# 16-bit threshold search on VectorE, matmul level ends and recount, and routing steps placed by a build-time estimate, in a gated scan with an eight-expert mixture

## The chip, the cores and the metric

The kernel runs on one core of one Trainium2 chip. The metric is the device time of one execution in microseconds. Before the change three runs took 1270.08, 1270.74 and 1274.23 us; the median is 1270.74 us. One further execution was taken with the profiler.

Five engines work from their own instruction queues: TensorE (PE, with its weight loads shown as PEld), VectorE (DVE), ScalarE (ACT), GpSimd (POOL) and SyncE (SP). An instruction waits on semaphores that other engines raise; whatever stands behind it on its engine waits too.

## The reference, cut to what matters

```python
def _attn_ref(x, f_logit, lower_bound):            # 4 x 5056 x 256
    f = lower_bound + (1 - lower_bound) * sigmoid(f_logit); i = 1.0 - f
    for t in range(S):
        h = f[:, t] * h + i[:, t] * x[:, t]
        y[:, t] = h

def _moe_ref(x, w_gate, w1, w2):                   # N = 20224 tokens, D 256, E 8, F 1024
    logits = x @ w_gate
    for idx in np.argsort(-logits.flatten()):      # greedy, best pair first
        tok, e = idx // E, idx % E
        if assigned[tok] >= 0 or counts[e] >= cap: # cap = N // E = 2528
            continue
        assigned[tok] = e; counts[e] += 1
    for e in range(E):
        out[assigned == e] = relu(x[assigned == e] @ w1[e]) @ w2[e]
```

A gated scan over 5056 steps gives 20224 token rows. Each token goes to one of eight experts. The assignment is greedy over all (token, expert) scores, with exactly 2528 places in each expert, so an expert's list is known only when the threshold is known at which it fills up.

## The kernel before

**Front.** The tokens come in 40 chunks of 512. `sig`, `fwd` and `back` do the sigmoid (ACT), the product with x (POOL), the transposes (PE, L518), the scan (DVE, L530) and the transposition back together with the gate scores (PE, L540 and L541). The rows are stored to a scratch buffer `hbuf` in DRAM by SP. `prep` takes, in small steps between the chunks, each token's best score `M0`, a one-hot `O` of its best expert, and two numbers `KH` and `KL` that hold the upper and the lower 16 bits of the score as a sortable integer.

**A route** (`route(k)`, eight of them) finds which expert fills up next and at which score. `search` does it in eight levels of base 16, four on `KH`, four on the rest `W`. A level has these steps:

- masks: for 160 columns of tokens and 16 thresholds, `MK[:, :, j, :]` says whether a token lies on the better side of threshold j. The 16 thresholds are shared out: DVE (L272) takes 8 to 13 of them, ACT (L308) five or six by a Sign activation each, POOL (L314) one to three in the first route;
- counts: 20 matmuls (L327) of `MK` with `O` add up, per threshold and expert, how many tokens there are;
- the level end: DVE takes the diagonal (`DM` L332, `CR` L333). In the first route two small matmuls follow (`CR` with `tot`, L346; a flag `fl` with `eighth`, L350). In all later routes DVE spreads `CR` to 128x128 (L354), one fp32r matmul (L357) adds it up, and three DVE steps (L359, L361, L362) make the digit. The last level of every route uses L335, L338, L340, L342;
- the next 16 thresholds `TH` (L366).

`assign` then marks the chosen tokens, `compact` turns the marks into a list of row numbers, eight groups of up to three blocks of 128 (matmuls L430, DVE L441 and L442, ACT `junk` L452, DVE `ids` L456; its PSUM tile has one buffer after the first route, so a group's matmuls wait for the ACT steps of the group before). `update` masks the filled expert in the scores (L464) and counts again how full every expert is: two comparisons (L467), two reductions (L471) and one matmul (L474). For the routes after the first, `argmax` and `keys` do again over 160 columns what `prep` did.

**The mixture.** `moe` goes through the experts in the order in which the routes find them. An expert's 20 tiles of 128 tokens form five chunks of four tiles, six (2, 4, 4, 4, 4, 2) for the first expert. For each chunk and each of eight blocks j of F, `first` does six matmuls into `pw` (L732; weights and tokens are split into a high and a low part) and ACT and DVE make `hh` (L737) and `hl` (L738); `second`, three blocks later, does 12 matmuls into `py` (L754). One block of a four-tile chunk is 6 + 12 matmuls. At a chunk's end ACT copies `y` (L760) and POOL scatters it to the output (L766). POOL also gathers the next tokens (`gather`, L704) and the next expert's weights (`load_w`, L657 and L658); `split` makes the weights' high and low parts (`w1h` L683, `w2s` L681 on ACT, `w1l` L689 on DVE). `trans` transposes the gathered tokens (L719, `xh`, `xl`).

**What sets the order.** The first route runs alone, with nothing to hide it but matmuls on zeros that keep PE busy (`busy`, L288; BZ says how many). The other routes run in the background of the mixture: `search` and the rest are generators that `yield` between steps, and `tick` is called once or twice in each `first` and between the tiles of a `second`. A tick advances each generator by at most one step. Before the change, each `yield` carries a letter, and the table `WAIT` (or `WAIT_1` for the first two routes) says how many ticks pass before the next step:

```python
WAIT = dict(a=2, k=0, m=2, c=6, d=2, z=1, g=0, f=0, s=4, p0=2, p1=1, p4=7, q0=5, q1=1, q2=7, u=3, w=0)
```

`gather(k + 1, 0)` stands in the second block of an expert's last chunk (GJ) and forces, by `ids_of`, as many steps of `compact` as its list still lacks; `gather(k + 1, 1)` stands four blocks later. The tile framework then schedules the instructions of the mixture on each engine; so the order of the queues is not exactly that of the calls, and is read from the built program below.

## Time and profile before

| | before |
|---|---|
| median of 3 runs | 1270.74 us (1270.08 to 1274.23) |
| the profiled execution's own time | 1270.02 us |
| its span, first to last instruction | 1268.2 us |
| PE, DVE, ACT, POOL busy | 1194.0, 826.9, 620.2, 487.7 us |
| front (scan), until the first route's counts | 0 to 157.8 us |
| first route and first weights, alone | 157.8 to 214.5 us |
| experts 0 to 4, with routes 1 to 6 in the background | 214.5 to 904.9 us: 156.8, 134.7, 133.3, 137.2, 128.4 |
| expert 5, with what is left of the routing | 904.9 to 1025.0 us: 120.1 |
| expert 6, no routing at all | 1025.0 to 1142.0 us: 117.0 |

The stretches begin with an expert's first matmul of L732. Some 1.8 us of the profiled execution's time lie outside its span. In the views a row gives start and length of an instruction, the engine, the line and the tiles (out<-in); what stands in brackets is the idle time before it and who ended that. "PEclk" is the TensorE clock that was granted: 1.00 is full speed, 0.50 is half. A busy PE is one that has a matmul in flight, which is not the same as one at its peak.

### The profile page before, as it was taken

The numbers are of one execution on the slowest core, as the hardware profiler recorded it, in microseconds if no ns is written. First come the engines' busy times: TensorE is split into PE (matmuls) and PEld (weight loads), VectorE is DVE, ScalarE is ACT, GpSimd is POOL, SyncE is SP. The second block draws the span as 40 slices with busy tenths as digits, with TensorE's granted clock in tenths as the row PEclk, the third lists the DMA queues.
The fourth block names the chain that finished last, engine by engine and source line by source line (L and its number), as shares of the span: only waits on it lengthen the run. The fifth ranks groups of instructions, "written<-read, shape, count | busy, mean of one in ns | idle before, by whom it ended". The sixth has DMA issues, their size and how long they took to land.

```text
span 1268.2 us, 23156 instructions
## 1 busy us (share of the span) xinstructions
PE 1194.0 (94%) x9062; PEld 1080.4 (85%) x9062; DVE 826.9 (65%) x1900; ACT 620.2 (49%) x1386; POOL 487.7 (38%) x467
## 2 busy tenths in 40 slices
PE   7999985999879989999989999999999999999998
PEld 7999964888778878888978888888888989999998
DVE  6999967778857787688679678868633352222222
ACT  7888733543455445355445545553644352322322
POOL 6677544512443242344243224333432342322312
PEclk9999996999889989999999999999999999999999
DMA  9999972201221211121131113112221111111100
GB/s 339 360 354 362 345 230 85 76 18 53 69 66 41 84 56 34 46 95 50 42 113 37 35 35 117 39 47 101 76 83 43 43 50 42 47 39 42 42 18 33
DMA packets 51725, 123.13 MB, mean 97 GB/s; under 512 B 7968, under 2 KB 28192, under 8 KB 50592
## 3 DMA queue, kind: packets, MB, share of 16 engines
q0 software_dynamic: 18816, 58.87, 14.7%
q1 hardware_dynamic: 32256, 62.78, 14.1%
q8 instruction: 71, 1.16, 0.4%
q14 instruction: 38, 0.31, 0.1%
q10 hardware_dynamic: 544, 0.01, 0.0%
HBM read 79.56 MB, written 42.07 MB: 96 GB/s over the span
## 4 chain that ended last, share of the span: by engine, by line
PE 47%; DVE 5%; ACT 2%; issue 1%; DMA 1%; POOL 0%; POOLq 0%; ACTq 0%; DVEq 0%
PE py L754 22%; PE pw L732 21%; DVE hl L738 1%; PE pt L719 1%; PE rt L327 1%; DMA r<-in_moe_w_dram,wi 1%; DVE w1l L689 1%; ACT w1h L683 1%; PE rt L430 0%; ACT hh L737 0%; ACT MK L308 0%; DVE w2s L687 0%; ACT junk L452 0%; DVE xl L723 0%; POOL out_dram L766 0%
## 5 line engine op out<-in xcount | busy, mean ns | idle before, releaser
L754 PE MATMUL py<-w2s,hh 128*128 128x256 f32 (+1 forms) x2560 | 493.7, 289 | 3.1 <-ACT y L760 3.1
L754 PEld LDWEIGHTS py<-w2s,hh 128*128 128x128 f32 (+1 forms) x2560 | 409.9, 189 | 28.6 <-issue 7.4
L738 DVE SCALAR_TENSOR_TENSOR hl<-pw,hh 128x512 fp32r<-128x512 f32 (+3 forms) x336 | 221.2, 658 | 292.7 <-ACT hh L737 270.8
L737 ACT ACTIVATE hh<-pw 128x512 fp32r<-128x512 f32 (+3 forms) x336 | 191.2, 569 | 435.6 <-PE pw L732 368.9
L754 PE MATMUL py<-w2s,hl 128*128 128x256 f32 (+1 forms) x1280 | 364.1, 284 | 0.7 <-issue 0.7
L766 POOL DMA_INDIRECT out_dram<-y,ids x160 | 166.2, 1039 | 433.5 <-ACT y L760 385.2
L732 PE MATMUL pw<-xl,w1h 128*128 128x512 f32 (+3 forms) x672 | 261.6, 389 | 3.1 <-DVE xl L723 3.1
L732 PE MATMUL pw<-xh,w1h 128*128 128x512 f32 (+3 forms) x672 | 260.0, 388 | 1.7 <-ACT xh L722 1.7
L732 PE MATMUL pw<-xh,w1l 128*128 128x512 f32 (+3 forms) x672 | 261.2, 389 | 0.0
L704 POOL DMA_INDIRECT xg<-hbuf,ids x160 | 172.7, 1079 | 211.5 <-PE pt L719 119.0
L754 PEld LDWEIGHTS py<-w2s,hl 128*128 128x128 f32 (+1 forms) x1280 | 242.1, 189 | 0.3 <-issue 0.2
L732 PEld LDWEIGHTS pw<-xh,w1l 128*128 128x128 f32 x672 | 129.4, 192 | 23.8 <-issue 0.8
L732 PEld LDWEIGHTS pw<-xl,w1h 128*128 128x128 f32 x672 | 129.4, 193 | 20.4 <-DVE xl L723 4.5
L732 PEld LDWEIGHTS pw<-xh,w1h 128*128 128x128 f32 x672 | 129.2, 193 | 15.1 <-ACT xh L722 2.3
L506 POOL TENSOR_TENSOR xl<-fl,xl 128x1024 f32<-128x1024 f32 (+1 forms) x40 | 94.6, 2366 | 39.9 <-ACT fl L505 28.9
L452 ACT ACTIVATE junk<-rt,r 128x158 bf16<-128x158 f32 x158 | 61.8, 391 | 78.2 <-DVE r L442 51.2
L530 DVE TENSOR_TENSOR_SCAN g<-fg,g,pb 128x512 f32<-128x512 f32 (+4 forms) x78 | 92.9, 1228 | 6.4 <-ACT fg L522 5.9
L540 PE MATMUL pr<-iw,g 128*128 128x136 f32 x316 | 62.7, 280 | 0.0
L541 PE MATMUL pr<-iw,g 128*128 128x136 f32 x316 | 62.5, 279 | 0.0
L522 ACT ACTIVATE fg<-pf,one,nomlb 128x512 f32<-128x512 f32 (+1 forms) x80 | 57.5, 769 | 2.3 <-PE pf L518 0.4
L327 PE MATMUL rt<-O,MK 128*128 128x64 bf16 x1120 | 43.5, 195 | 13.8 <-POOL MK L314 8.7
L327 PEld LDWEIGHTS <-MK 128*128 128x128 bf16 x1120 | 36.7, 99 | 23.2 <-POOL MK L314 10.9
(203 smaller groups left out, 1481.2 us busy)
## 6 DMA issues: line engine op xcount, KB each, us to landing
hbuf<-hr SPq DMA_DIRECT2D x39, 528.0 KB, 9.1
fl<-in_f_logit_dram SPq DMA_DIRECT2D x39, 512.0 KB, 6.0
xl<-in_x_dram SPq DMA_DIRECT2D x39, 512.0 KB, 6.3
xg<-hbuf,ids POOLq DMA_INDIRECT x160
out_dram<-y,ids POOLq DMA_INDIRECT x160
r<-in_moe_w_dram,wi POOLq DMA_INDIRECT x24
hbuf<-hr SPq DMA_DIRECT2D x1, 264.0 KB, 9.2
fl<-in_f_logit_dram SPq DMA_DIRECT2D x1, 256.0 KB, 6.0
```

What stands on the lines that cost most here:

```text
L327: nc.tensor.matmul(ps[:, :64], MK[:, g], O[:, 8 * g:8 * g + 8, :], start=(g == 0), stop=(g == NG - 1))
L452: last = nc.scalar.activation(junk, p3[:, b, :NT], AF.Sign, bias=r[:, 0, b:b + 1], scale=-1.0, accum_out=r[:, 1, b:b + 1])
L506: nc.gpsimd.tensor_mul(XT[i][:np_], FT[i][:np_], XT[i][:np_])
L530: nc.vector.tensor_tensor_scan(GT[i][:, h, c:e], f[:, h, c:e], pb[h][:, c:e], init, op0=OP.mult, op1=OP.add)
L540: nc.tensor.matmul(pr[:, :P + E], g[:, 0], iw[:, :P + E], start=True, stop=False, skip_group_check=True)
L541: nc.tensor.matmul(pr[:, P:], g[:, 1], iw[:, P + E:], start=False, stop=True, skip_group_check=True)
L704: st = nc.gpsimd.indirect_dma_start(out=XG[k, c][:n, q].bitcast(F32), out_offset=None, in_=hbuf, in_offset=ids_at(k, c, q, n))
L732: nc.tensor.matmul(ps[:, :w], a[:, h, j], b[:, h, :w], start=(i == 0), stop=(i == 5))
L737: nc.scalar.activation(hh[:, :w], ps[:, :w], AF.Relu)
L738: v.scalar_tensor_tensor(hl[:, :w], ps[:, :w], 0.0, hh[:, :w].bitcast(F32), op0=OP.max, op1=OP.subtract)
L754: nc.tensor.matmul(py, x, w, start=(j == 0 and i == 0 and q % 2 == 0), stop=(j == FB - 1 and i == 2), skip_group_check=True)
L766: st = nc.gpsimd.indirect_dma_start(out=out, out_offset=ids_at(k, c, r, n), in_=y[:n, r % 2], in_offset=None)
```

## The change

**16-bit keys and thresholds, all masks on VectorE.** The key's upper half is kept as int16 (`K16`), the rest as int16 (`R16`), and the thresholds as an int16 tile of 16 x 8 in which each threshold stands eight times. A level's masks become two DVE instructions of 1280 elements each (80 columns, 16 thresholds), with int16 in and bfloat16 out. ACT and POOL make no masks any more. In the last level threshold 0 is done apart, in fp32 (`wth`). `TH` and `PRE` grow from 16 to 128 elements. Two more DVE steps make `R16` from `W` once per search.

**Short level end.** All routes use the two small matmuls (`CR` with `tot`, `fl` with `eighth`); the spread to 128x128, its fp32r matmul and the three DVE steps behind it go, save in the last level.

**Recount by matmuls.** `update` counts how many tokens lie above the threshold by 20 matmuls of the marks `SB` with `O` and one small matmul, in place of the two comparisons and two reductions.

**Steps issued by an estimate.** `Pace` keeps, while the program is built, an estimate of when each engine is free and each tile ready. A generator's `yield` names an engine and the tiles that the next step needs; a tick takes the step only when the estimate says that the tiles are ready by the time the engine is free, and that this engine is at most 3 us (SLACK) behind PE. The wait tables go. The weight split starts 30 ticks after `load_w`, not 40, with 8 ticks between its pieces unless the next expert is near. Since every call goes through a helper, all instructions have the line L100 in the changed kernel.

```diff
+    def cost(self, eng, op, out, ins, accum):
+        n = self.cols(out)
+        if eng == "PE":
+            moving = ins[-1]
+            if moving.dtype == F32:
+                return 1.71 * n + 4 if op == "matmul" else 0.85 * n
+            return max(29.0, 0.453 * n + 4) if moving.dtype == F32R else max(29.0, n / 2.4 + 2.5)
...
+        if eng == "DVE":
...
+            if all(x.dtype in (BF, I16) for x in (out, *ins)):
+                n /= 2
+            return 145 + 1.045 * n * (2 if "scan" in op else 1) + 80 * accum
+        return 1000.0 if "dma" in op else 200 + 2.3 * n
...
+    def due(self, eng, tiles, slack):
+        now = self.free["PE"]
+        at = max(now, self.free[eng])
+        return at - now <= slack and all(self.ready.get(self.key(t), 0.0) <= at for t in tiles)
...
+    def masks(val, th, c0, c1, j0=0):
         n = (c1 - c0) // 8
+        v.tensor_tensor(MK[:, c0 // 8:c1 // 8, j0:, :],
                         val[:, c0:c1].rearrange("p (g c) -> p g c", c=8).unsqueeze(2).to_broadcast(
+                            [P, n, 16 - j0, 8]),
+                        th[:, j0:].unsqueeze(1).to_broadcast([P, n, 16 - j0, 8]), op=OP.is_ge)
...
-    BZ = [18, 5, 12, 42]
+    BZ = [11, 5, 12, 42]
...
-                    for i in range(3):
-                        for j in ac[2 * i:2 * i + 2]:
-                            nc.scalar.activation(MK[:, :, j, :], val.rearrange("p (g c) -> p g c", c=8), AF.Sign,
-                                                 bias=th[:, j:j + 1], scale=-1.0)
...
+                    for c in (0, 80):
+                        if c and not first:
+                            yield 'DVE',
+                        masks(val, th, c, c + 80, 1 if last else 0)
+                        if last:
+                            v.tensor_scalar(MK[:, c // 8:c // 8 + 10, 0, :],
+                                            W[:, c:c + 80].rearrange("p (g c) -> p g c", c=8), wth, None, op0=OP.is_le)
...
+                yield 'PE', CR
+                nc.tensor.matmul(ps[:, 64:64 + E], tot_v, CR, start=True, stop=True)
+                yield 'DVE', ps
+                v.tensor_scalar(FL, ps[:, 64:64 + E], 0.0, 0.0, op0=OP.is_ge, op1=OP.max, accum_out=fl)
+                yield 'PE', fl
+                nc.tensor.matmul(ps[:, 80:81], eighth, fl, start=True, stop=True)
...
+        if first:
+            v.tensor_scalar(TR, A1, code, None, op0=OP.is_equal)
+            v.scalar_tensor_tensor(MS, W, tlo, TR, op0=OP.is_lt, op1=OP.mult, accum_out=cS)
+        else:
...
-        for e in (0, 4):
-            with nc.allow_low_precision(reason=EXACT):
-                v.tensor_reduce(Qb[:, e:e + 4], TMP[:, :, e:e + 4].rearrange("p c e -> p e c"), AX.X, OP.add)
-            yield 'u'
         ps = rt.tile([P, 512], F32, name="rt")
-        nc.tensor.matmul(ps[:, :E], ones_b, Qb, start=True, stop=True)
+        for g in range(NG):
+            nc.tensor.matmul(ps[:8, :64], SB[:, 8 * g:8 * g + 8], O[:, 8 * g:8 * g + 8, :], start=(g == 0),
+                             stop=(g == NG - 1))
...
-    WAITW, WS_ = 40, 2
+    WAITW, WAITS, SLACK = 30, 8, 3000.0
```

Three places in the queues. On DVE, in the first route, one level from the thresholds to the next `DM`, before:

```order
L366 SCALAR_TENSOR_TENSOR TH<-rt,PRE 128x16
L272 TENSOR_TENSOR MK<-KH,TH 128x20x72
L319 TENSOR_SCALAR PRE<-jt_122,TH 128x16
L332 TENSOR_TENSOR DM<-rt,bm 128x64
L333 TENSOR_REDUCE CR<-DM 128x8
```

and after, the same level:

```order
L100 SCALAR_TENSOR_TENSOR TH<-rt,PRE 128x128
L100 TENSOR_TENSOR MK<-K_168,TH 128x1280 x2
L100 SCALAR_TENSOR_TENSOR PRE<-TH,njt_121 128x128
L100 TENSOR_TENSOR DM<-rt,bm 128x64
L100 TENSOR_REDUCE CR<-DM 128x8
```

The one mask instruction with 9 of 16 thresholds has become two with all 16, each for half of the columns; the six instructions on ACT and POOL beside it are gone.

On PE, at the first block of expert 0's last chunk (the one whose matmuls are 128x224), before. `rt` is a group of the list of expert 1, `g1` its mask:

```order
L732 MATMUL pw_4490<-xh_4315,w1l_2951 128x224
L732 MATMUL pw_4490<-xh_4315,w1h_2950 128x224
L732 MATMUL pw_4490<-xl_4316,w1h_2950 128x224
L430 LDWEIGHTS g1_4444
L430 MATMUL rt_4486<-RA_187,g1_4444 128x160
```

and after, at the second block of the same chunk:

```order
L100 MATMUL pw_4319<-xh_4087,w1l_2840 128x224
L100 MATMUL pw_4319<-xh_4087,w1h_2839 128x224
L100 LDWEIGHTS g1_4280
L100 MATMUL rt_4326<-RA_186,g1_4280 128x160
L100 LDWEIGHTS g1_4280
```

Before, this is the fourth group of the list (`rt_4230`, `rt_4312` and `rt_4405` stand earlier, in the chunk of 512); after, it is the first. The next groups after (`rt_4344`, `rt_4396`, `rt_4482`) stand 10, 13 and 39 matmuls of the mixture behind one another.

On ACT, where expert 1's weights are split, before:

```order
L737 ACTIVATE hh_4209<-pw_4202 128x512
L683 ACTIVATE w1h_4377<-r1_4166,omlb_101 128x512 x4
L737 ACTIVATE hh_4237<-pw_4226 128x512
L681 ACTIVATE w2s_4379<-r2_4167 128x2x256 x2
L452 ACTIVATE junk_4255,r_4254<-rt_4230,r_4254 128x158
```

and after:

```order
L100 ACTIVATE hh_4203<-pw_4193 128x512
L100 ACTIVATE w1h_4243<-r1_4211,omlb_101 128x512 x4
L100 ACTIVATE hh_4239<-pw_4232 128x512
L100 ACTIVATE w2s_4245<-r2_4212 128x2x256 x4
L100 ACTIVATE hh_4303<-pw_4294 128x224
L100 ACTIVATE junk_4336,r_4335<-rt_4326,r_4335 128x158
```

Before, fifteen blocks of expert 0 come behind the first piece of the split; after, nine, eight of them in the short last chunk, and all eight pieces stand ahead of the first `junk` step of expert 1's list.

342 lines of the change are left out of this document (181 added, 161 removed).

## The prediction

> **What bounds the kernel now.** I read the table of stretches first, cut at each expert's first matmul; its columns are length, busy time (and instructions) of PE, PEld, DVE, ACT and POOL, granted clock, DMA share, GB/s.
>
> ```profile
> 214.50:371.30 156.80, 139.48 (x1041) 124.73 (x1042) 119.70 (x301) 73.11 (x194) 56.64 (x53) 0.92 0.18 55
> 371.30:506.00 134.70, 128.66 (x984) 113.98 (x983) 101.04 (x252) 68.29 (x174) 44.45 (x43) 0.97 0.17 54
> 506.00:639.30 133.30, 128.12 (x1018) 114.40 (x1017) 101.14 (x244) 67.92 (x168) 47.94 (x45) 1.00 0.18 57
> 639.30:776.50 137.20, 130.09 (x983) 115.40 (x982) 104.42 (x263) 63.14 (x152) 49.55 (x48) 0.98 0.22 68
> 776.50:904.90 128.40, 125.77 (x964) 112.41 (x963) 99.17 (x249) 65.66 (x166) 46.49 (x43) 1.00 0.19 60
> 1025.00:1142.00 117.00, 116.10 (x762) 105.46 (x761) 40.67 (x60) 40.44 (x69) 40.76 (x40) 1.00 0.15 46
> ```
>
> PE carries the mixture. Expert 6, with no routing beside it, takes 117.0 us. Experts 0 to 4 take 690.4 us where five times 117.0 is 585.0, so background routing costs 105 us of PE's time although DVE is busy for only about 75% of these stretches. The waits of PE between 214.5 and 904.9 us say what it stood for (total, times, longest):
>
> ```profile
> PE rt L430 <- ACT junk L452: 6.6, 6, 1.9
> PE rt L474 <- DVE Qb L471: 5.3, 3, 3.1
> PE rt L357 <- DVE ZR L354: 5.1, 5, 1.7
> PE rt L413 <- DVE RS L409: 3.7, 3, 3.2
> PE py L754 <- ACT y L760: 3.1, 2, 2.9
> PE rt L327 <- DVE MK L272: 2.5, 2, 1.5
> PE rt L357 <- DVE CR L333: 1.8, 3, 0.8
> PE pw L732 <- ACT xh L722: 1.7, 2, 1.1
> PE rt L327 <- ACT MK L308: 1.3, 1, 1.3
> ```
>
> These hold 31 us, most of it for routing matmuls that reached the head of PE's queue before the step in front of them was done; the mixture's matmuls stood behind them. The third view is the clock, in the five stretches of this stage where it was cut:
>
> ```profile
> 214.70:224.90 10.20, 8.18 (x38) 7.52 (x38) 8.82 (x24) 3.25 (x11) 6.54 (x5) 0.50 0.19 52
> 323.90:330.70 6.80, 5.79 (x24) 4.88 (x24) 5.43 (x15) 4.34 (x11) 4.20 (x4) 0.50 0.18 61
> 358.00:368.30 10.30, 8.88 (x63) 8.33 (x61) 4.67 (x15) 5.32 (x18) 4.11 (x5) 0.67 0.20 68
> 460.40:467.20 6.80, 6.34 (x23) 5.61 (x24) 5.96 (x18) 3.29 (x11) 5.12 (x5) 0.50 0.22 78
> 661.80:668.60 6.80, 5.21 (x19) 4.71 (x19) 5.40 (x13) 5.77 (x9) 2.59 (x3) 0.50 0.52 182
> ```
>
> Length times the missing share of the clock is 5.1 + 3.4 + 3.4 + 3.4 + 3.4 = 18.7 us. So the 105 us are about 31 of long waits, 19 of clock, and 55 of routing's own matmuls and small gaps. The front, up to 157.8 us, is not touched: the page's slices show the DMA queues full there, and what `prep` saves on DVE lies under the loads.
>
> **The first route, alone on the chip (157.8 to 214.5 us).** Nothing hides it, so each step counts. One level of the timeline, from the thresholds to the next diagonal:
>
> ```profile
> 167.59 0.17 DVE L366 SCALAR_TENSOR_TENSOR TH<-rt,PRE 128x16 f32<-128x16 f32 x1 [0.25 <-PE rt L350]
> 167.80 1.66 DVE L272 TENSOR_TENSOR MK<-KH,TH 128x1440 bf16<-128x1440 f32 x1
> 167.86 1.70 ACT L308 ACTIVATE MK<-KH,TH 128x160 bf16<-128x160 f32 x5 [3.08 <-DVE TH L366]
> 167.93 2.07 POOL L314 TENSOR_SCALAR MK<-KH,TH 128x160 bf16<-128x160 f32 x1 [2.65 <-DVE TH L366]
> 170.06 0.76 PE L327 MATMUL rt<-O,MK 128*128 128x64 bf16 x20 [0.52 <-POOL MK L314]
> 170.86 0.23 DVE L332 TENSOR_TENSOR DM<-rt,bm 128x64 f32<-128x64 f32 x1 [1.11 <-PE rt L327]
> ```
>
> POOL's single threshold ends last, and the 20 matmuls follow: 3.23 us from the start of `TH` to their end. After the change DVE makes two masks of 1280 elements. The trace has no 16-bit instruction with two inputs, so I bound one mask. At the pace of the fp32 masks above (1.66 us for 1440) it takes 1.48 us. The other end is the fastest that DVE goes in this program, where one input is compared with a column:
>
> ```profile
> L422 DVE TENSOR_SCALAR g<-IO,st 128x384 bf16<-128x384 f32 x40 | 16.6, 416 | 0.0
> L359 DVE TENSOR_TENSOR GP<-rt,rE 128x128 f32<-128x128 f32 x42 | 12.1, 288 | 26.4 <-PE rt L357 14.5 <-PE pw L732 9.6 <-PE rt L430 2.0
> L422 DVE TENSOR_SCALAR g<-IO,st 128x128 bf16<-128x128 f32 x8 | 2.2, 278 | 0.0
> L383 DVE TENSOR_TENSOR asg<-asg,TI 128x160 f32<-128x160 f32 x7 | 2.2, 316 | 0.0
> ```
>
> 256 more elements cost 138 ns, 0.54 ns each, so 1280 cost 0.278 + 1152 x 0.00054 = 0.90 us. The row nearest by operation is the fp32 mask, but what the change alters is just what separates the two: half the bytes per element, and thresholds laid out so that no input repeats one element along its innermost run. I take 0.90 us. [...]
>
> A level then is 0.21 us to the masks, 0.11 more because `TH` has 128 elements (row L359, 0.288, against 0.17), 1.80 for two masks, 0.06 to PE, and 0.38 for the second ten matmuls, the first ten running under the second mask: 2.56 us, 0.67 less. With slow masks it is 3.72, 0.49 more. Six levels: -4.0 (slow +2.9). The fewer filler matmuls (18 to 11) end before the masks do and cost nothing. `R16` adds two steps of the kind of row L383: +0.6. `assign` loses two such steps: -0.6. The last level:
>
> ```profile
> 192.50 4.16 POOL L314 TENSOR_SCALAR MK<-W,TH 128x160 bf16<-128x160 f32 x3 [2.74 <-DVE TH L366]
> 196.71 1.25 PE L327 MATMUL rt<-O,MK 128*128 128x64 bf16 x20 [4.69 <-POOL MK L314]
> ```
>
> Three thresholds on POOL and 20 matmuls are 5.5 us from 192.50. After, 0.11 for `TH`, 0.17 for `wth`, two masks of 1200 elements with a piece of 80 each (0.86 + 0.28 at most) and ten matmuls at half clock: 3.2 us, -2.3 (slow -1.2). Sum of this stage: **-6.3 us** (slow +1.7). The stores of the scratch rows do not come late for it, since the page's slices show the DMA queues with room there.
>
> **The background routes.** Five terms, against the 105 us.
>
> *Waits that the change addresses*: L474 5.3 (the recount no longer waits for two reductions), L357 5.1 + 1.8 (the step is gone), L327 2.5 + 1.3, L413 3.7: 19.7 us, and some 1 us of shorter ones. PE now meets these steps when the estimate has them ready. The estimate doesn't see a full PSUM ring, a late DMA or a half clock, so I let a fifth stay: **-17** (0 to -21).
>
> *New work on PE*: seven recounts of 20 matmuls, each about 0.6 us (the 0.76 above less the last one's passage), 4; and in 42 levels a pair of small matmuls in place of one, which on the lone path takes
>
> ```profile
> 171.45 0.39 PE L346 MATMUL rt<-CR,tot 128*128 128x8 f32 x2
> ```
>
> and beside full matmuls I put at 0.1 more than the one removed, 4: **+8** (4 to 20).
>
> *The change of experts 0 to 1 and 1 to 2.* With the steps paced, expert 1's list is begun only in expert 0's short last chunk, behind the whole weight split on ACT. Rows of a split in expert 2, and of a block's matmuls:
>
> ```profile
> 541.35 0.97 POOL L657 DMA_INDIRECT r<-in_moe_w_dram,wi  x1 [4.24 <-DVE wi L379]
> ...
> 549.72 0.97 POOL L658 DMA_INDIRECT r<-in_moe_w_dram,wi  x1 [0.30 <-issue]
> ```
>
> ```profile
> 545.75 2.48 ACT L683 ACTIVATE w1h<-r,omlb 128x512 fp32r<-128x512 f32 x2 [0.95 <-DMA r<-in_moe_w_dram,wi]
> ...
> 557.49 2.19 ACT L681 ACTIVATE w2s<-r 128x512 fp32r<-128x512 f32 x4 [1.54 <-DMA r<-in_moe_w_dram,wi]
> ```
>
> ```profile
> 592.81 1.45 PE py L754 x12
> 608.16 1.44 PE pw L732 x6
> ```
>
> The last of three loads starts 2.6 us after the first (1.3 us from one issue to the next), lands 7.8 us later (549.72 to 557.49), and ACT's four pieces take 2.2: 12.6 us until ACT reaches the first `junk`, about 15 until both are through with the `hh` between them. PE has two blocks of 2.9 us and two of about 2 us in the short chunk before the second group: some 10 us. So it stands 5 us there. A third group, 13 matmuls (1.5 us) behind, waits 1 more, and the gather (four issues of 1.3 us, then landing) ends about 4 us after PE asks for its transposes. That is 10 us; at the next change two groups are forced, each at most the longest 1.9 us of row L430, 4. Before, half of row L430's 6.6 us was these same groups' waits (a choice): **+10.7** (0 to 22).
>
> *Clock.* The cuts at 323.9, 358.0 and 661.8 us follow waits that go, the first this one:
>
> ```profile
> 324.91 0.17 PE L474 MATMUL rt<-Qb,onesb 128*128 128x8 bf16 x1 [3.09 <-DVE Qb L471]
> ```
>
> So -10.2, and one new cut of 6.8 us at the change of experts, +3.4: **-6.8** (-13.6 to +3). [...]
>
> *ACT and POOL without masks.* The 252 mask steps on ACT in this stage (six routes of seven levels, six in each) are gone from ahead of `hh`, `y` and `xh`; of rows L760, L722 and the other half of L430 (8 us) I take half: **-4** (0 to -8).
>
> Sum: -17 + 8 + 10.7 - 6.8 - 4 = **-9.1 us**. What DVE saves beyond this (argmax and keys are unchanged) lies under PE's work. Expert 5, beside which only the end of routing runs, I leave as it is.
>
> **The time.** The profiled execution took 1270.02 us: 1270.0 - 6.3 - 9.1 = 1254.6; the median of the runs is 0.7 above it, so **1255 us**.
>
> **Rivals.**
>
> *More is gained.* If the change of experts hides under the mixture and all cuts of the clock but the first go, the terms are -17 + 8 + 0 - 13.6 - 4 and -6.3: **1238 us**. For it: each cut follows a single long wait. Against: the order on ACT puts eight weight pieces ahead of the first `junk`.
>
> *Nothing is gained.* The change of experts costs twice what I put (21.4) and brings two more cuts (6.8): **1272 us**. The gathers stand behind scatters on POOL, and each late gather delays the next expert's first block. It decides from about 15 us of PE's idle time beyond mine at the first two changes.
>
> *The steps don't come as estimated.* The tile framework schedules anew: the split, 8 ticks apart by the estimate, stands as four and four in a row on ACT. If routing matmuls are moved likewise, the 17 us stay: **1272 us**.
>
> *Slower: masks at one element per pace step.* The estimate reckons 0.81 us for a mask (145 + 1.045 x 640 ns). At 1.48 us each level's two masks end 1.3 us after PE has been told; over 48 levels that is 64 us, of which I let the spacing of the ticks hide half. The first route adds 1.7 in place of -6.3: 1255 + 32 + 8 = **1295 us**. It decides above some 1.1 us per mask. For it: every two-input row of this trace goes at the slow pace. Against: none of them has 16-bit inputs.
>
> **How the numbers follow.** My forecast (1242 to 1266 by its own bounds) gets 0.57, more gain 0.18, nothing gained 0.10, another order 0.05, slow masks 0.10. The range 1232 to 1275 holds nearly all of the forecast, half of the first rival and most of the second and third, close to 8 in 10; slow masks lie outside. About 0.3% (4 us) is what a measurement of this kernel can tell from no change. Faster by more: 0.57 + 0.18 less a tail, 0.73. Within: 0.15. Slower: 0.12.
>
> **What would show it.** In the profile after: `MK` rows of 1280 elements at 0.8 to 0.9 us, not 1.5; first route to first expert matmul near 50 us, not 56.7; experts 2 to 4 at 124 to 130 us with few waits of `rt` matmuls; expert 0 no better than about 150 us, with waits for `junk` and a cut of the clock before expert 1. It is wrong if experts 2 to 4 stay above 133, or if the first change of experts shows no wait of several us.

## The result, and the profile after

Nine runs of the changed kernel had a median of 1289.0 us (1283.8 to 1292.9), nine of the kernel before beside them 1274.0 us (1270.1 to 1279.4). The ratio is 1.0116, with a 95% interval of 1.0089 to 1.0142: slower by 1.2%, where 1.2% faster was forecast. The profiled execution took 1289.05 us, its span 1287.3 us, so the profile is that of a median run. The profile of before is of an execution at 1270.0 us, so some 4 of the 19.1 us between the two spans are not the change's: the medians lie 15.0 apart.

The stretches of after, cut as those of before (front, first route, experts 0 to 5); columns are length, busy time (and instructions) of PE, PEld, DVE, ACT and POOL, granted clock, DMA share, GB/s:

```profile
0.00:162.60 162.60, 148.92 (x1273) 145.83 (x1274) 142.88 (x238) 131.86 (x219) 105.25 (x107) 1.00 0.98 341
162.60:212.90 50.30, 33.53 (x372) 25.62 (x369) 35.60 (x121) 8.28 (x14) 6.67 (x7) 0.83 0.63 200
212.90:358.40 145.50, 134.00 (x1052) 119.31 (x1053) 97.88 (x257) 52.71 (x126) 47.72 (x48) 0.95 0.18 55
358.40:495.20 136.80, 129.86 (x972) 112.57 (x972) 82.90 (x214) 50.30 (x115) 42.04 (x42) 0.97 0.17 53
495.20:646.00 150.80, 139.00 (x1066) 120.11 (x1065) 90.10 (x239) 52.84 (x117) 52.28 (x48) 0.94 0.18 54
646.00:784.80 138.80, 133.87 (x1059) 117.08 (x1058) 88.47 (x238) 52.74 (x117) 46.41 (x43) 0.99 0.17 54
784.80:919.20 134.40, 130.75 (x1042) 115.86 (x1041) 90.85 (x248) 49.74 (x109) 49.03 (x45) 1.00 0.19 60
919.20:1044.10 124.90, 122.77 (x828) 110.58 (x827) 53.32 (x148) 59.50 (x150) 44.62 (x45) 0.99 0.22 72
```

Against before (158.0, 56.5; 156.8, 134.7, 133.3, 137.2, 128.4, 120.1) the front is 4.6 us longer, the first route 6.2 shorter, and the six experts together take 831.3 us where they took 810.5: 20.8 more. Only expert 0 is shorter; expert 2 is 17.5 longer. Experts 6 and 7 are unchanged.

I split the 20.8 us by the distance from the start of each matmul to the next: what is usual for its shape is work; more than 0.15 us beyond that is a stall; the missing share of the clock is told apart. Routing matmuls took 57.2 us of PE for 42.7 (+14.5), stalls 40.3 for 42.9 (-2.6), the clock 23.8 for 18.7 (+5.1), and the rest is short gaps (+3.8).

**The stalls changed place.** PE's waits in experts 0 to 4 (total, times, longest):

```profile
PE rt L100 <- issue: 8.8, 7, 3.7
PE rt L100 <- ACT junk L100: 7.6, 4, 5.8
PE rt L100 <- DVE CR L100: 5.1, 5, 1.8
PE pt L100 <- issue: 3.7, 2, 3.2
PE pw L100 <- ACT xh L100: 3.6, 2, 2.4
PE rt L100 <- DVE FL L100: 3.2, 3, 1.7
PE rt L100 <- DVE Z L100: 2.4, 3, 1.7
```

The waits for masks and for the recount are gone, and that for `RS` is 0.5 us. In their place stand the two visits of the level's end (`CR`, `FL`), and "issue", where the view names no releaser. By PE's idle time right in front of each matmul, in experts 0 to 5, those behind masks, `ZR`, `Qb` and `RS` lost 21.0 us before, and `RS` alone loses 0.5 now. But `CR`, `fl` and `Z` lose 14.4, of it 12.0 at `CR` and `fl`, where `ZR` had lost 7.3; 4.5 are lost inside a mask group; and the list's groups (`RA`) lose 9.2 for 8.1.

**More work on PE.** The groups of the new matmuls (busy, mean ns of one, idle before them):

```profile
L100 PE MATMUL rt<-CR,tot 128*128 128x8 f32 x98 | 16.4, 239 | 10.0 <-DVE CR L100 6.4 <-issue 3.7
L100 PE MATMUL rt<-fl,eighth 128*128 128x1 bf16 x49 | 8.6, 175 | 3.8 <-DVE FL L100 3.8
L100 PE MATMUL rt<-O,SB 128*8 128x64 bf16 x140 | 5.7, 200 | 0.0
```

`CR` with `tot` is two matmuls per level. Between full matmuls the pair holds PE for 0.22 us and the flag's for 0.04, where `ZR` held it for 0.06.

**The clock** was cut seven times in experts 0 to 5, mostly at gaps of PE that add up to 1.6 us or more. One of these gaps stands behind the forced groups of expert 1's list:

```profile
333.75 0.40 PE L100 MATMUL py<-w2s,hh 128*128 128x256 f32 x2
339.93 0.43 PE L100 MATMUL rt<-RA,g 128*128 128x160 bf16 x2 [5.78 <-ACT junk L100]
```

PE stands from 334.2 to 339.9 us, and has half its clock from 336.2 to 343.1.

**Signals came late while POOL issued DMAs.** The worst case, on all engines:

```profile
618.03 1.13 POOL L100 DMA_INDIRECT xg<-hbuf,ids  x1 [8.66 <-PE rt L100]
...
621.32 0.76 PE L100 MATMUL rt<-O,MK 128*128 128x64 bf16 x20
...
621.98 1.00 POOL L100 DMA_INDIRECT out_dram<-y,ids  x1 [0.30 <-ACT hh L100]
...
623.28 0.99 POOL L100 DMA_INDIRECT out_dram<-y,ids  x1 [0.31 <-issue]
624.57 0.97 POOL L100 DMA_INDIRECT out_dram<-y,ids  x1 [0.30 <-issue]
625.85 0.97 POOL L100 DMA_INDIRECT out_dram<-y,ids  x1 [0.30 <-issue]
626.73 0.22 DVE L100 TENSOR_TENSOR DM<-rt,bm 128x64 f32<-128x64 f32 x1 [4.25 <-remote]
...
627.32 0.60 PE L100 MATMUL rt<-CR,tot 128*128 128x8 f32 x2 [3.67 <-issue]
```

The mask matmuls end at 622.08, DVE is free from 622.49, and `DM` starts 4.25 us later; PE stands behind it. The median delay of `DM`, from the end of the group or of what DVE did before, is 0.04 us. It is over 0.3 us in 20 of 56 levels, 28.1 us in all (before: 9, 11.0 us), and always with an indirect DMA on POOL within the last 1.5 us or still running: of 26 levels with one, 20 are late, of 30 without, none. POOL stood 8.7 us for a list just before this burst. DMAs in bursts of six or more number 87 after and 69 before, the longest bursts 16 and 8.

**The front.** DVE's and POOL's rows at two places:

```profile
52.80 2.28 DVE L100 COPY K<-K 128x32 int16<-128x32 int16 x1
58.71 2.33 DVE L100 TENSOR_SCALAR KH<-K 128x32 f32<-128x32 int16 x1
```

```profile
52.69 2.36 POOL L100 TENSOR_TENSOR xl<-fl,xl 128x1024 f32<-128x1024 f32 x1 [0.67 <-ACT fl L100]
58.46 2.54 POOL L100 TENSOR_TENSOR xl<-fl,xl 128x1024 f32<-128x1024 f32 x1
```

```profile
L100 DVE TENSOR_SCALAR KH<-K x12: 166/224/2332, 58.7 to 835.3; 128x160 f32<-128x160 int16 x6, 128x32 f32<-128x32 int16 x4, 128x16 f32<-128x16 int16 x1, 128x14 f32<-128x14 int16 x1
```

Two conversions of 32 elements per partition, in the median 0.22 us (the third view, by tile: shortest, median and longest in ns), end with POOL's product that began just before them, 0.03 and 0.04 us behind its end: 4.2 us of DVE's time.

### The profile page after: what moved, and what is told of

The parts are those of the page before. It is cut to its first block, busy times and chain, and to the rows that moved or that the text cites. A ratio compares the mean times of both kernels' runs of the same rounds, so it can differ in the third digit from the quotient of the medians.

```text
span 1287.3 us, 23122 instructions
## 1 busy us (share of the span) xinstructions
PE 1208.9 (94%) x9244; PEld 1083.6 (84%) x9244; DVE 756.5 (59%) x1813; ACT 534.6 (42%) x1104; POOL 464.8 (36%) x452
## 3 DMA queue, kind: packets, MB, share of 16 engines
q0 software_dynamic: 18816, 58.87, 14.5%
## 4 chain that ended last, share of the span: by engine, by line
PE 45%; issue 4%; DVE 2%; POOL 2%; ACT 1%; DMA 1%; POOLq 0%; ACTq 0%
PE py L100 21%; PE pw L100 20%; PE rt L100 2%; DMA r<-in_moe_w_dram,wi 1%; PE pt L100 1%; POOL out_dram L100 1%; ACT w1h L100 1%; POOL xg L100 1%; DVE hl L100 0%; ACT hh L100 0%; DVE w1l L100 0%; DVE TMP L100 0%; ACT junk L100 0%; DVE CR L100 0%; ACT y L100 0%
## 5 line engine op out<-in xcount | busy, mean ns | idle before, releaser
L100 PE MATMUL py<-w2s,hh 128*128 128x256 f32 (+1 forms) x2560 | 494.1, 290 | 2.3 <-ACT y L100 1.8
L100 PEld LDWEIGHTS py<-w2s,hh 128*128 128x128 f32 (+1 forms) x2560 | 408.6, 189 | 26.5 <-issue 7.7
L100 ACT ACTIVATE hh<-pw 128x512 fp32r<-128x512 f32 (+3 forms) x336 | 191.6, 571 | 554.7 <-PE pw L100 416.2
L100 DVE SCALAR_TENSOR_TENSOR hl<-pw,hh 128x512 fp32r<-128x512 f32 (+3 forms) x336 | 220.5, 656 | 311.7 <-ACT hh L100 287.3
L100 PE MATMUL py<-w2s,hl 128*128 128x256 f32 (+1 forms) x1280 | 364.6, 285 | 0.1
L100 POOL DMA_INDIRECT out_dram<-y,ids x160 | 168.4, 1052 | 406.9 <-ACT y L100 368.5
L100 PE MATMUL pw<-xl,w1h 128*128 128x512 f32 (+3 forms) x672 | 262.8, 391 | 1.5 <-DVE xl L100 1.2
L100 PE MATMUL pw<-xh,w1h 128*128 128x512 f32 (+3 forms) x672 | 259.4, 387 | 3.9 <-ACT xh L100 3.6
L100 PE MATMUL pw<-xh,w1l 128*128 128x512 f32 (+3 forms) x672 | 263.0, 391 | 0.0
L100 POOL DMA_INDIRECT xg<-hbuf,ids x160 | 165.0, 1031 | 267.9 <-PE pt L100 82.4
L100 PEld LDWEIGHTS py<-w2s,hl 128*128 128x128 f32 (+1 forms) x1280 | 242.2, 189 | 0.3 <-issue 0.3
L100 PEld LDWEIGHTS pw<-xh,w1l 128*128 128x128 f32 x672 | 129.3, 192 | 21.7 <-issue 0.4
L100 PEld LDWEIGHTS pw<-xh,w1h 128*128 128x128 f32 x672 | 128.7, 192 | 15.5 <-ACT xh L100 4.7
L100 PEld LDWEIGHTS pw<-xl,w1h 128*128 128x128 f32 x672 | 128.9, 192 | 15.1 <-DVE xl L100 2.7
L100 ACT ACTIVATE junk<-rt,r 128x158 bf16<-128x158 f32 x158 | 61.9, 392 | 118.7 <-DVE r L100 105.1
L100 POOL TENSOR_TENSOR xl<-fl,xl 128x1024 f32<-128x1024 f32 (+1 forms) x40 | 94.8, 2369 | 40.7 <-ACT fl L100 32.2
L100 DVE TENSOR_TENSOR_SCAN g<-fg,g,pb 128x512 f32<-128x512 f32 (+4 forms) x78 | 92.8, 1228 | 11.4 <-ACT fg L100 10.0
L100 PE MATMUL pr<-iw,g 128*128 128x136 f32 x632 | 79.9, 280 | 0.0
L100 PEld LDWEIGHTS pr<-iw,g 128*128 128x128 f32 x632 | 76.2, 191 | 0.1
L100 ACT ACTIVATE fg<-pf,one,nomlb 128x512 f32<-128x512 f32 (+1 forms) x80 | 57.5, 768 | 2.4 <-PE pf L100 0.4
L100 POOL DMA_INDIRECT r<-in_moe_w_dram,wi x24 | 25.9, 1080 | 86.6 <-DVE wi L100 37.2
L100 DVE TENSOR_TENSOR xl<-pt,xh 128x512 fp32r<-128x512 f32 (+1 forms) x80 | 54.0, 675 | 3.5 <-ACT xh L100 3.0
## 6 DMA issues: line engine op xcount, KB each, us to landing
fl<-in_f_logit_dram SPq DMA_DIRECT2D x39, 512.0 KB, 5.6
xl<-in_x_dram SPq DMA_DIRECT2D x39, 512.0 KB, 6.0
```

What stands on the lines that cost most here:

```text
L100: r = f(*args, **kw)
```

## The experiments

My theory on reading the traces: the first route is as forecast; the front lost to the conversions; in the background the level's end waits twice, and POOL, held up by late lists, then issues in bursts beside which signals come late. The rivals: new PE work explains it; or the pacing itself makes routes and lists longer. Ratios are to the kernel before, run on the same chip; the other columns are of the profiles. The last column counts the steps of `compact` that a gather forced after expert 0, in the program's order.

A profile is of one execution, and the profiles come from several chips, on which the kernel before had medians from 1268.5 to 1274.0 us. In the background conversions_on_pool has the instructions of after, and still its profile is 9.5 us shorter there. So a difference of under some 10 us between two profiles shows nothing by itself; the ratios, with their intervals, decide.

| kernel | ratio (95%) | front | first route | experts 0 to 5 | clock / stalls | forced |
|---|---|---|---|---|---|---|
| before | 1 | 158.0 | 56.5 | 810.5 | 18.7 / 42.9 | 0 |
| after | 1.0116 (1.0089 to 1.0142) | 162.6 | 50.3 | 831.3 | 23.8 / 40.3 | 26 |
| level_end_vectore | 0.9809 (0.978 to 0.9838) | 156.8 | 49.4 | 789.5 | 6.8 / 25.6 | 21 |
| recount_vectore | 1.0079 (1.0053 to 1.0105) | 162.1 | 50.8 | 822.1 | 23.5 / 41.3 | 37 |
| conversions_on_pool | 1.0061 (1.0039 to 1.0083) | 157.0 | 49.3 | 821.8 | 20.1 / 35.5 | 26 |
| no_scatter | 0.996 (0.9941 to 0.998) | 161.9 | 49.8 | 800.1 | 13.6 / 21.3 | 26 |
| extra_visit | 1.0114 (1.0075 to 1.0152) | 156.8 | 49.9 | 826.1 | 22.1 / 42.6 | 70 |
| room_600 | 1.0236 (1.0217 to 1.0255) | 164.4 | 50.0 | 833.8 | 21.9 / 48.4 | 71 |
| fixed_waits | 0.9957 (0.9935 to 0.998) | 162.1 | 49.6 | 804.6 | 8.5 / 28.8 | 0 |
| all_three | 0.9983 (0.9969 to 0.9997) | 156.4 | 49.9 | 811.8 | 19.8 / 45.1 | 36 |
| lists_by_ticks | 0.999 (0.9973 to 1.0008) | 164.5 | 50.4 | 814.1 | 16.6 / 31.2 | 5 |
| slack_8 | 0.9961 (0.9947 to 0.9975) | 162.7 | 49.8 | 809.9 | 11.9 / 31.8 | 0 |
| end_and_ticks | 0.9848 (0.9822 to 0.9873) | 155.9 | 48.8 | 799.8 | 6.5 / 34.5 | 0 |
| masks_alone | 0.9791 (0.9772 to 0.981) | 157.0 | 50.0 | 795.7 | 10.2 / 35.0 | 0 |
| paced_masks_8 | 0.9875 (0.9858 to 0.9893) | 157.7 | 49.6 | 803.9 | 14.6 / 41.6 | 8 |
| paced_end_8 | 0.988 (0.983 to 0.9929) | 157.4 | 49.4 | 798.2 | 9.4 / 31.4 | 0 |

**level_end_vectore.** The long level end of before is put back in the routes after the first; masks, recount and estimate stay.

```diff
+                    v.tensor_tensor(ZR, CR.unsqueeze(1)..., selv.unsqueeze(2)..., op=OP.mult)
+                    yield 'PE', ZR
+                    nc.tensor.matmul(ps[:, 64:192], ones_r, ZR..., start=True, stop=True)
...
-                yield 'PE', CR
-                nc.tensor.matmul(ps[:, 64:64 + E], tot_v, CR, start=True, stop=True)
```

> The kernel after, with the end of a level in the background routes as it was before (one fp32r matmul and three VectorE steps in place of two small PE steps); the first route, masks, recount and pacing stay. Theory A (what the change puts on PE is paid in full, and each of its two PE steps per level meets a late VectorE step now and then): 42 levels lose 0.20 us of PE each, 8.4 us, and some 4 of the 14 us of waits ahead of these steps go with the second visit: 1289 - 12 = 1277 us, routing matmuls on PE down from 57 to 49 us. Theory B (pacing is at fault: the estimate gives VectorE too little room, so 1.1 us more of VectorE per level makes more waits): 1289 to 1297 us with the waits ahead of the level's end above 14 us.

It is 3.0% faster than after, some 39 us. In the profiles, which here differ by more than the ratios say, 5.8 us come in the front (where no conversion meets POOL's product any more) and 41.8 in experts 0 to 5; routing matmuls take 8.2 us less, and a route 108.3 us for 118.5. Its third expert:

```profile
477.70:613.30 135.60, 130.76 (x1068) 116.27 (x1066) 99.07 (x269) 52.58 (x126) 49.15 (x47) 1.00 0.20 58
```

Here 135.6 us at full clock; in after 150.8 at 0.94. The level's end carries far more than the 12 us that I expected. But 18 signals are still late, 27.7 us in all, as in after: late signals alone don't cost the time.

**recount_vectore.** The two comparisons and two reductions of `update` are put back.

```diff
-            nc.tensor.matmul(ps[:8, :64], SB[:, 8 * g:8 * g + 8], O[:, 8 * g:8 * g + 8, :], ...)
+                v.tensor_reduce(Qb[:, e:e + 4], TMP[:, :, e:e + 4].rearrange("p c e -> p e c"), AX.X, OP.add)
```

> The kernel after, with the recount by VectorE reductions and one matmul as before, but paced; all else stays. Theory A: 7 recounts give back 0.86 us of PE each, 6 us, and no wait comes back since PE is told of the step only when the reductions are reckoned done: 1283 us. Theory B (without the short recount PE meets the reductions early again): the 5 to 6 us of wait of before come back and the time stays at 1288 to 1290 us.

0.4% less than after, but the two intervals overlap. By the profiles it is 9.2 us in the background, of which only the recount's matmuls, 5.9, can be told from noise. Stalls and clock stay.

**conversions_on_pool.** The three conversions of `prep` go to POOL.

```diff
-        v.tensor_copy(K16[:, c0:e], half(k1, 1))
+        nc.gpsimd.tensor_copy(K16[:, c0:e], half(k1, 1))
```

> The kernel after, with the three small conversions of keys in the front (16-bit keys, their float copies) on POOL in place of VectorE. Theory A (two of these conversions stood 2.3 us each behind POOL's multiply of 2.36 us, which held what both engines need): none stands there any more, the front ends 4.6 us earlier (first search matmul at 158 and not at 162.6 us), 1284.5 us. Theory B (the front is late because of its added instructions or by chance of the loads): the first search matmul stays within 1 us of 162.6 and the time at 1288 to 1290 us.

Its front, and one conversion, by the stretches and by tile:

```profile
0.00:157.00 157.00, 147.79 (x1272) 145.48 (x1273) 137.33 (x223) 131.73 (x219) 109.28 (x122) 1.00 1.00 352
```

```profile
L100 POOL TENSOR_SCALAR KH<-K x6: 211/331/389, 56.3 to 159.2; 128x32 f32<-128x32 int16 x4, 128x16 f32<-128x16 int16 x1, 128x14 f32<-128x14 int16 x1
```

The front is 5.6 us shorter, no conversion takes over 0.39 us, and the ratio falls by 0.55%, 7 us. So the front's 4.6 us were these conversions; that the product held what both engines need is my reading of where the rows end, no more. The other kernels agree: the seven in which two conversions of over 2.2 us stand in the front, after among them, have fronts of 161.9 to 164.5 us, and the eight without have 155.9 to 157.7. In five of these eight the conversions are on DVE as in after, and merely fall elsewhere in time.

**no_scatter.** The scatters of experts 0 to 6 are left out, so these rows of the output are not written.

```diff
-                for r in (q - 1, q):
+                for r in (q - 1, q) if k == E - 1 else ():
```

> The kernel after without the scatters of the results of experts 0 to 6 (those rows of the output are not written); the gathers and all else stay. Theory A (while POOL issues indirect DMAs, PE's signals reach VectorE and ACT up to 4 us late, and a paced PE step with 0.4 us of room then waits): signals from the mask matmuls to VectorE that are over 0.3 us late fall from 20 of 56 (28 us in all) to under 10 (under 12 us), PE's waits and cuts of the clock fall by half, and the time by 12 to 20 us, to 1269 to 1277. Theory B (the late starts have nothing to do with POOL's issues): about 20 late starts stay and the time is within 4 us of 1289.

Experts 1 and 2:

```profile
352.50:478.00 125.50, 125.50 (x974) 110.70 (x973) 81.35 (x213) 49.62 (x113) 25.24 (x26) 1.00 0.14 41
478.00:616.70 138.70, 134.83 (x1066) 117.80 (x1065) 90.01 (x239) 52.67 (x117) 27.54 (x26) 0.98 0.13 38
```

With the same routing on PE (57.2 us) stalls fall by 19 us and the clock's loss by 10; 8 signals are late, 7.4 us in all, for 20 and 28.1. PE is busy all through expert 1. What POOL does beside PE matters then for late signals and stalls, though this takes waiting and issuing away together. As many steps are forced as in after.

**extra_visit.** level_end_vectore with a second visit to PE in each level: the flag's matmul and two small DVE steps, one on each side of it, that change nothing in the digit.

```diff
+                    v.tensor_scalar(FL, GP[:, 0, :], 0.0, 0.0, op0=OP.is_ge, op1=OP.max, accum_out=fl)
+                    yield 'PE', fl
+                    nc.tensor.matmul(ps[:, 200:201], eighth, fl, start=True, stop=True)
+                    yield 'DVE', ps
+                    v.tensor_tensor(GP[:, 0, 0:1], GP[:, 0, 0:1], ps[:, 200:201], op=OP.min)
```

> The run level_end_vectore with one more PE visit in every level of the background routes, which changes no number: a small VectorE reduction, one bf16 matmul of one column (0.04 us of PE), and a VectorE step that needs it. Theory A2 (a paced PE step costs by being one more place where PE can stand behind a late VectorE step, and the longer chain brings the next expert's list later; its own matmul hardly counts): a good part of the 40 us comes back, 0.990 to 1.005 of the kernel before, with the clock cut in more than one place after 350 us. Rival (the 40 us were the fp32 matmuls of the level's end, 0.22 us a pair, and what they delay): within 4 us of the run level_end_vectore, 0.981 to 0.985.

It puts 0.8 us of work on PE, and the ratio goes from 0.9809 to 1.0114. 70 steps are forced for 21; expert 5 takes 143.1 us for 120.6, since routing runs into it (219 routing matmuls for 38). Here the cost isn't work but a second meeting with PE: a route takes 126.8 us for 108.3, of which the two DVE steps, 0.4 us in each of seven levels, are less than 3; and the lists come late.

**room_600.** After, with 600 ns added to when the estimate takes a tile for ready, on PE's steps.

```diff
-        ... all(self.ready.get(self.key(t), 0.0) <= at for t in tiles)
+        ... all(self.ready.get(self.key(t), 0.0) + (600.0 if eng == "PE" else 0.0) <= at for t in tiles)
```

> The kernel after, where the estimate issues a PE step only when its input was reckoned ready 0.6 us before, in place of just ready. Theory A (PE stands because the steps come with no room): waits ahead of CR, fl and Z matmuls fall from 18 to about 9 us, half of the cuts of the clock go with them, and the time is 6 to 15 us below the kernel after (1.000 to 1.007 of the kernel before). Rival (room makes the routes longer, 3 visits x 8 levels x 0.6 us is 14 us per route, and the lists are then forced at the change of experts): same as the kernel after or slower, with waits ahead of the RA matmuls above 8 us.

If too small a margin were the whole fault, this would mend it. It is 1.2% slower than after: the routes stretch from 118.5 to 131.6 us each. Its waits:

```profile
PE rt L100 <- DVE MS L100: 7.6, 2, 5.9
PE rt L100 <- issue: 7.4, 9, 1.9
PE pt L100 <- DMA xg<-hbuf,ids: 5.0, 4, 2.9
PE rt L100 <- DVE CR L100: 3.7, 4, 1.2
```

The margin does mend the waits of the level's end: by the idle time in front of each matmul, `CR`, `fl` and `Z` cost 4.8 us for 14.4. But forced lists (`MS`, 7.6 for 2.7) and late gathers (`xg`) come instead.

**fixed_waits.** After with fixed waits in ticks in place of the estimate.

```diff
-                if not pace.due(self.need[0], self.need[1:], SLACK):
-                    return
-                self.wait = self.apart
+                self.wait = self.apart or wait_of(self.need)
+    WAIT = {"": 2, "ps": 1, "MK": 6, "CR": 1, "Z": 1, "fl": 0, "cnt": 4, "RS": 2, "RA": 7, "SB": 3, "r": 1}
```

> The kernel after, with its steps spaced by before's fixed numbers of ticks in place of the estimate; masks, level end and recount stay as after. Theory A (pacing does its part: it took away 4 us of waits ahead of the mask matmuls, 6 ahead of the recount and 3 to 4 ahead of the first list matmul): these come back and the time is 5 to 20 us above the kernel after. Theory B (pacing is what makes the kernel slower): below the kernel after by 10 us or more, near 1.000 of the kernel before.

1.6% faster than after with the same instructions, some 20 us (by the profiles 26.7 us less in experts 0 to 5). Its row of waits for `CR` is longer than that of after, not shorter:

```profile
PE rt L100 <- DVE CR L100: 10.3, 12, 1.8
```

But the row holds the closing pair of the recount too. By the idle time in front of each matmul, the level's end (`CR` with `tot`, and `fl`) costs 6.8 us for 12.0, and the recount's pair 6.1 us, where after has none. No wait for `junk` is left, nothing is forced, and the clock costs 8.5 us for 23.8. A route takes 105 us for 118.5. With the instructions of after, the estimate is what makes the kernel slower than before; with the long level end (level_end_vectore) the same estimate doesn't.

**all_three.** Long level end, old recount, conversions on POOL, with the estimate: in the background, the masks alone, paced.

```diff
+        nc.gpsimd.tensor_copy(K16[:, c0:e], half(k1, 1))
+                    nc.tensor.matmul(ps[:, 64:192], ones_r, ZR..., start=True, stop=True)
+                v.tensor_reduce(Qb[:, e:e + 4], TMP[:, :, e:e + 4].rearrange("p c e -> p e c"), AX.X, OP.add)
```

> The kernel after with the end of a level on VectorE in the background, the recount on VectorE and the front's conversions on POOL. Theory A (each gives its own share): the 6 us of the recount come on top of the run level_end_vectore, which had the front early already: 0.976 of the kernel before, 1239 us where that takes 1269. Rival (with the level's end short of PE work PE no longer pays for the recount, or its longer VectorE chain makes the lists late): 0.980 to 0.985.

A miss for every theory: the gains don't add. With the old recount the paced kernel loses 22.3 us in experts 0 to 5 against level_end_vectore, though PE has 6 us less to do; 36 steps are forced for 21, and 101 DMAs go in bursts of six or more for 63.

**lists_by_ticks and slack_8.** Two ways to get lists early with the estimate kept: `compact` alone by ticks; or the limit of 3 us raised to 8.

```diff
+                if self.gen.__name__ != "compact" and not pace.due(self.need[0], self.need[1:], SLACK):
+                self.wait = wait_of(self.need) if self.gen.__name__ == "compact" else self.apart
```

> The kernel after, with only the steps of the lists (compaction) spaced by before's fixed ticks; the routes stay paced by the estimate. In program order the steps of lists that a gather forces after expert 0 fall from 26 to 5. Theory C (the paced lists are not ready when their gathers come to the head of POOL's queue; POOL stands, then issues 10 to 17 indirect DMAs without a pause, PE's signals arrive 1 to 4 us late meanwhile, and the clock is cut): bursts of at least 6 fall from 87 DMAs to under 65, experts 1 and 2 lose 15 us, and the time is 1.000 or less of the kernel before. Rival (the routes' own paced steps, with no room, are what costs): 1.007 to 1.013.

```diff
-    WAITW, WAITS, SLACK = 30, 8, 3000.0
+    WAITW, WAITS, SLACK = 30, 8, 8000.0
```

> The kernel after, where the estimate lets VectorE's queue run 8 us ahead of PE in place of 3. No list step is forced after expert 0, in program order. Theory C: as in the run lists_by_ticks, 1.000 or less of the kernel before, with expert 2 near 135 us and not 151. Rival (a longer VectorE queue puts hl behind routing steps, and PE then waits ahead of the py matmuls): these waits rise from 5 to over 15 us and the time stays above 1.005.

Both take much of the loss back: 1.2% and 1.5%. In lists_by_ticks expert 2 falls to 134.4 us but expert 1 rises to 146.4, so the two lose 6.8 us together, not the 15 that I expected. slack_8 also lets the routes' own steps go earlier (a route takes 109.5 us). Its expert 2:

```profile
497.80:630.10 132.30, 130.54 (x1038) 114.73 (x1037) 89.47 (x233) 49.90 (x109) 45.94 (x43) 1.00 0.18 57
```

132.3 us at full clock for 150.8. With nothing forced this paced kernel is as fast as fixed_waits (0.9961 and 0.9957): here the estimate then does no harm, and gains nothing.

**end_and_ticks and masks_alone.** Without the estimate: long level end, matmul recount and conversions on POOL; then long level end and old recount, with the conversions on DVE. Both have the edits of fixed_waits and level_end_vectore; the third part is that of conversions_on_pool or of recount_vectore. masks_alone keeps more of the change than the masks: the shorter making of the keys, the earlier weight split, and one table of waits in place of two.

```diff
+                self.wait = self.apart or wait_of(self.need)
+    WAIT = {"": 2, "ps": 1, "MK": 6, ..., "SB": 3, "r": 1, "ZR": 1, "Qb": 3}
+                    nc.tensor.matmul(ps[:, 64:192], ones_r, ZR..., start=True, stop=True)
```

> The kernel after with the end of a level on VectorE in the background, the front's conversions on POOL, and all steps by before's fixed ticks: only masks, first route and recount of the change stay. Theory A and C together: the run fixed_waits (0.9957) less 8 us of PE work and 5 us of the front: 0.985 of the kernel before or less, 1250 where that takes 1269. Rival (fixed ticks and the VectorE level's end do not add, since a level's chain is longer on VectorE): 0.990 to 0.996.

> Of the change only the 16-bit keys, masks and thresholds with the shorter first route: the end of a level in the background, the recount and the spacing of the steps are those of before. Theory A (these parts gain by themselves: 6 us in the first route, and PE's work stays as it was): 0.985 to 0.995 of the kernel before if the front is not held. Rival (VectorE now carries the masks of ACT and POOL and is late for PE, so that what the first route gains is lost): 0.996 to 1.005.

end_and_ticks came as expected (0.9848 for 0.985). masks_alone, 2.1% faster than before and better than the 0.985 to 0.995 expected, beats both kernels and is the fastest of all by its median ratio, though its interval overlaps that of level_end_vectore. It keeps the waits that the rest of the change was made for:

```profile
PE rt L100 <- DVE ZR L100: 9.4, 12, 2.7
PE rt L100 <- DVE Qb L100: 3.5, 3, 2.0
PE rt L100 <- DVE MK L100: 2.8, 3, 1.4
```

**paced_masks_8 and paced_end_8.** The instructions of masks_alone, and of level_end_vectore, with the estimate and the limit of 8 us (so the first also has the old recount).

```diff
+    WAITW, WAITS, SLACK = 30, 8, 8000.0
+                    nc.tensor.matmul(ps[:, 64:192], ones_r, ZR..., start=True, stop=True)
```

> The instructions of the run masks_alone (level's end and recount on VectorE, 16-bit masks), with the estimate and a limit of 8 us for VectorE's queue in place of fixed ticks. In program order 8 list steps are forced after expert 0. Theory D (the estimate loses by late lists alone and its placing of PE steps has a worth of its own): 0.970 to 0.977 of the kernel before, with waits ahead of MK, ZR and Qb below 15 us where masks_alone has 22. Theory E (its placing is worth nothing, since a signal that comes 1 to 4 us late is not in the estimate): 0.978 to 0.985, the same as masks_alone or slower.

> The run level_end_vectore with a limit of 8 us in place of 3; no list step is forced after expert 0, in program order (21 there). Theory D (late lists are what the limit costs): at least as fast as level_end_vectore, 0.970 to 0.980 of the kernel before; and the level's end then costs 0.9961 (slack_8) less this and less 0.005 for the front, some 12 us. Theory E (the limit does not matter by itself, level_end_vectore was fast because its bursts of DMA happened to be short): 0.981 to 0.990.

Pacing with early lists costs masks_alone 0.9%, more than either theory held. For level_end_vectore the larger limit brings no gain (0.988 for 0.9809) though nothing is forced any more: that speaks against late lists as the whole cost of the limit.

## Why the prediction was wrong

**The step that failed** is the first of the background: "PE now meets these steps when the estimate has them ready", with only a fifth of 20.7 us to stay, -17. The waits named there did go: PE idled 21.0 us in front of `MK`, `ZR`, `Qb` and `RS`, and idles 0.5 now. But 14.4 us stand in front of `CR`, `fl` and `Z`, 4.5 inside a mask group, and `RA` costs 1.1 more, so nothing is left of the gain. Experts 2 to 4 took 150.8, 138.8 and 134.4 us, above the 133 that the prediction named as the sign of being wrong. I had counted what was removed and given the two new meetings at the level's end no waits of their own, only PE time. I also took the limit of 3 us for harmless. It makes routes longer (118.5 us each, 109.5 with a limit of 8, 105 with ticks; 111 before), and then lists are forced at changes of expert that were free before. That it takes the estimate and the second visit together is shown: without the estimate the same instructions are 0.4% faster than before (fixed_waits), and with the estimate and one visit 1.9% faster (level_end_vectore). The way in which they cost is shown in part only. For late lists speak slack_8 and lists_by_ticks, which force few steps or none and mend much, and room_600 and extra_visit, which force 71 and 70 and are slow. Against them as the whole of it: no_scatter gains 1.5% with as many forced steps as after, and level_end_vectore is fast with 21. Nor are the waits at the level's end the whole: room_600 takes two thirds of them away and is slower still.

**What each part did**, built up with ticks, in experts 0 to 5: before 810.5, masks_alone 795.7, matmul recount 799.8, short level end 804.6, estimate 831.3. So -14.8, +4.1, +4.8, +26.7, in this order; the two small ones are within what profiles of the same instructions differ by. The ratios of the whole time are 0.9791, 0.9848, 0.9957 and 1.0116, with no two intervals overlapping (the third step also puts the conversions back on DVE). It isn't a sum that holds in any order. With the limit of 3 us the estimate costs masks_alone's instructions 1.9% (all_three), with the matmul recount nothing that is clear of noise (level_end_vectore 0.9809, end_and_ticks 0.9848, whose intervals overlap), and with the short level end too 1.6%.

**Term by term.**

- First route -6.3: measured -6.2, right. One level in the views of after:

```profile
167.01 0.29 DVE L100 SCALAR_TENSOR_TENSOR TH<-rt,PRE 128x128 int16<-128x128 f32 x1 [0.26 <-PE rt L100]
167.34 1.56 DVE L100 TENSOR_TENSOR MK<-K,TH 128x1280 bf16<-128x1280 int16 x2
...
168.96 0.46 PE L100 MATMUL rt<-O,MK 128*128 128x64 bf16 x10
...
169.46 0.22 DVE L100 TENSOR_TENSOR DM<-rt,bm 128x64 f32<-128x64 f32 x1 [0.36 <-PE rt L100]
```

  From `TH` to the end of the counts are 2.41 us (forecast 2.56, before 3.23); a mask takes 0.82 us (taken: 0.90). That excludes the slow masks. From 256 to 1280 elements a 16-bit mask grows by 0.53 ns per element, where the fp32 masks of before grow by 1.04 (from 640 to 1440 elements).
- "Front not touched": wrong, +4.6. I had weighed only how much DVE does there, not beside which POOL instruction it falls.
- New PE work +8: +14.5. The pair of fp32 matmuls costs 0.16 us more than what it replaces, and the flag's 0.04, over 42 levels 8.4; I had put 0.1 in all. A recount costs 0.89 with its closing pair, seven of them 6.2, for 4.
- Change of experts +10.7: the first was as told. PE stands 5.8 us behind `junk` and 3.2 at the transposes, 9 for 10, and the clock is cut there twice. At the second, no `junk` is waited for; PE stops in the middle of a mask group instead:

```profile
495.64 0.44 PE L100 MATMUL rt<-O,MK 128*128 128x64 bf16 x7
497.22 0.28 PE L100 MATMUL rt<-O,MK 128*128 128x64 bf16 x4 [1.14 <-issue]
497.94 0.19 PE L100 MATMUL rt<-O,MK 128*128 128x64 bf16 x1 [0.45 <-issue]
499.36 0.25 PE L100 MATMUL rt<-O,MK 128*128 128x64 bf16 x3 [1.22 <-issue]
500.79 0.21 PE L100 MATMUL rt<-O,MK 128*128 128x64 bf16 x1 [1.17 <-issue]
```

- Clock -6.8: +5.1. The three cuts whose waits I removed went, and others came with the new waits.
- ACT and POOL without masks -4: masks_alone brings 14.8 us. I had counted only the waits that name ACT. Stalls fall by 7.9 and the clock's loss by 8.5 (short gaps rise by 1.6), so as much as I had put down to the estimate comes without it. Whether the masks bring all of it, or the earlier split and the new table some, wasn't tried.

**The rivals.** "Nothing is gained" (1272) was nearest of those with 16-bit masks at full pace. Its mechanism, late lists and late DMAs on POOL and more cuts of the clock, is part of what happened; the level's end and the front, which it didn't hold, make the rest. Slow masks (1295) lay nearest by the number alone, and the masks weren't slow. "The steps don't come as estimated" is false in its form: after the start of expert 0, PE's order in the built program is that in which the steps were issued, with two exceptions; they come in the order, but not at the time.

**What stays open.** Why signals of PE reach DVE late while POOL issues indirect DMAs, and why PE stops inside a group where the profile shows nothing that it waits for: both fall beside such DMAs (the trace has no instruction load between 494.1 and 512.0 us, nor between 613.1 and 635.3). Taking POOL's DMAs off another way was not tried. Open, too, is why level_end_vectore, with 21 forced steps and 27.7 us of late signals, is as fast as masks_alone. My guess is that it matters where a burst falls; no run shows it.

## What to carry to other kernels

Count the meetings between engines that a change adds, not only their work: here each took a wait of its own beside a busy engine (12.0 us for the two of a level's end), and made the rounds longer under a rule that holds steps back until they are reckoned ready. Look then for a deadline downstream (here a gather) that forces what comes late. Build such a change up one part at a time; here the first of four steps held all the gain. Look also at what a small step on VectorE runs beside: here two of 0.22 us in the median took 2.28 and 2.33 us, as the GpSimd product beside them lasted 2.36 and 2.54, while in five of the kernels that left them on VectorE none took over 2.2.
